# PSUM seeds in two blocks only, five staging buffers, earlier stores of differences, a merge over eight banks, and fetches issued one by one

## The chip, the cores and the metric

The kernel runs on one core of a Trainium2 chip. The metric is the time of one execution on the device, in microseconds (us), as the median of three runs. A profile of one more execution supplies everything else. The engines are TensorE (PE; PEld is its weight load), VectorE (DVE), ScalarE (ACT), GpSimd (POOL) and SyncE (SP). SP only issues DMAs here, and ACT issues some beside its computing. Each engine works through its own instruction list strictly in order, so an instruction that waits holds up all that stand behind it.

## The reference

A retention layer feeds two gated layers; all is in float32, for 3,072 tokens of 512 features.

```python
for t in range(S):
    state = gamma * state + einsum('bhd,bhe->bhde', k[:, :, t], v[:, :, t])
    y[:, :, t] = scale * einsum('bhd,bhde->bhe', q[:, :, t], state)
x = y.transpose(0, 2, 1, 3).reshape(3072, 512)
x = ((x @ w1) * (x @ w2) @ w3) @ w_out            # 512 -> 1024 -> 1024 -> 512
h = maximum(maximum(x @ u1, x @ u2), x @ u3)      # 512 -> 768
out = h @ u_out                                   # 768 -> 512
```

## The kernel before

Each matrix product is done by a seven-product scheme (Strassen's, in the Winograd form): an operand is cut into quarters, seven sums of quarters are multiplied, and sums of the seven products give the four quarters of the result. Each factor is split into a rounded value and a remainder (`hi`, `lo`), and three matmuls (hi·hi, hi·lo, lo·hi) make one product to near float32 accuracy. Those are the three lines L495, L496, L497, which always come together.

The stages in order of time, with their place in the profile: attention (0 to 88 us); the first gate, `x @ w1` times `x @ w2` (88 to 332, lines 473 to 545); the merge of `w3` and `w_out` into one matrix (332 to about 382, `merge_mm`); the product with it, "the x stage" (to 494, lines 640 to 690); the second gate with its maximum (494 to 763, lines 735 to 815); the last product.

**The first gate** runs over six blocks: two groups `g` of output columns, and in each the three token sets `n`; `blk = g * NB + n`. A block has seven steps `q`, and a step has four groups `p` of six matmuls into one PSUM bank each, so a block has 168 matmuls. `s = 7 * blk + q` counts the steps. `sets_b` gives the eight banks two names: set `a` takes steps 0, 2, 4, 6 and set `b` takes 1, 3, 5, and the two change places from block to block. Each group's result is taken out of PSUM after its last matmul:

```python
if q == 0:
    nc.scalar.copy(out=sets["b"][p] if blk else u, in_=ps)
elif seeded:
    nc.scalar.copy(out=u, in_=ps)
elif q == 1:
    nc.vector.tensor_tensor(out=u, in0=u, in1=ps, op=ALU.add)
```

So in block 0 step 0 is copied to the SBUF tile `U`, and step 1 is added to it by DVE (L504). In later blocks step 0 is copied by ACT (L500) into the banks that step 1 uses next, step 1 accumulates on top of it (a "seed"), and ACT copies the finished sum to `U` (L502). Steps 2 and 3 are copied to `C` and `E` by ACT (L506, L508), steps 4, 5 and 6 are combined by DVE (L510, L512, L517), and POOL multiplies `C` by `U` (L513). In steps 0 and 1 of the next block `fsums` forms four differences (`z` 0 to 3) of the finished quarters on DVE (L239), and `store` puts each on a list that `stores()` sends at the end of the step, from SP, to the scratch tensor `fsp`. Until such a store has landed, L506 and L508 may not overwrite `C` and `E`.

**Weights** come as 64-bit numbers and are turned into float32 on the chip. `fetch` starts the DMA of one weight tile (512 KB) into one of three staging tiles `stg`, and `step` alternates `decode_a` and `decode_b`: ACT L117, POOL L119, DVE L140 and L142, ACT L149, DVE L128 (or L134), ACT L130, DVE L108. A staging tile is free after L108 (L134), and only then `due_more` issues the next fetch, from ACT's queue (`late`). `Spread` deals these steps out evenly over the groups of a block, by `side.tick()`. `wgen` (lines 197 to 222) makes the seven sums of the second column group's weights, one at the end of each of seven steps, from step `s = 14 + LAG` on. `make_op` prepares the left operands in blocks 0 to 2; from block 3 on they are reloaded from the scratch tensor `opsp` by ACT's DMAs (L486, 1 MB each), three steps ahead.

**The merge** writes product `z` into `bank[z % 4]`, and two ACT copies (L586) take it out. **The second gate** has three rounds `j` of three blocks. Its operands are reloaded by L633, its seeds are L787, and at the start of a round `more(3)` starts three fetches for the next round.

Before each stage `more(3)` fills the three staging tiles.

Of the kernel before, what the change touches and what calls it, by code (L numbers as in the profile page):

```python
# [32 lines left out]
GA = 4  # L33
# [7 lines left out]
NSTG = 3  # L41
# [6 lines left out]
def fused_kernel(ctx: ExitStack, tc: tile.TileContext, ck, w12, w3t, wo1, w123, wo2, mask, gout, gch, kdec, out):  # L48
    nc = tc.nc
# [12 lines left out]
    fsp = dram.tile([NB, 7, 2, P, 2 * N], F32, name="fsp")  # L62
# [16 lines left out]
    stage_turn = [0]  # L79
    loaded, fronts, pending, wq = [], [], [], []  # L80

    def fetch(src, raw, hi=None, lo=None, st=None):
        k = stage_turn[0]
        stage_turn[0] += 1
        st = stg[k % NSTG][:, :] if st is None else st
        (nc.scalar if late[0] else nc.sync).dma_start(out=st.bitcast(I64), in_=src)
        loaded.append((st, dec_t[k % 2][:, :], raw, hi, lo))
# [81 lines left out]
    def store(dst, src, wait=1):  # L169
        later.append([wait, dst, src])  # L170
# [64 lines left out]
    def fsums(n, g, z):  # L235
        c, e = (work[nm] for nm in "CE")
        x00, x10, x01, x11, t = c[:, :1024], c[:, 1024:], e[:, :1024], e[:, 1024:], s_t[:, :]
        o, a, b, q = ((x00, x01, x00, 4), (t, x11, x00, 2), (x01, x11, x01, 3), (x10, t, x10, 5))[z]
        nc.vector.tensor_tensor(out=o, in0=a, in1=b, op=ALU.subtract)  # L239
        store(fsp[n, q, g], o, 0)  # L240

# [151 lines left out]
    with tc.manual_schedule():  # L393
# [72 lines left out]

        LAG = 3
        PB = (-1, -1, -1, -1, -1, -1, -1)
        wq += [lambda i=i, u=u: fetch_w12(i, u) for u in range(2) for i in range(GA, KF)]
        more(3)  # L470
        side = Spread([idle] * 5 + [step] * (4 * GA), 4 * (14 + LAG))
        wgen = weights(raw_quads(1024), 1024)
        for g in range(KF // GA):
            for n in range(NB):
                blk = g * NB + n
                sets = sets_b(blk)
                for q in range(7):
# [11 lines left out]
                    w = wslot(q).rearrange("p h (i k n) -> p h i k n", i=GA, k=2)  # L489
                    seeded = blk > 0 and q == 1  # L490
                    for p in range(GA):
# [7 lines left out]
                        if q == 0:  # L499
                            nc.scalar.copy(out=sets["b"][p] if blk else u, in_=ps)  # L500
                        elif seeded:
# [14 lines left out]
                        else:  # L516
                            nc.vector.tensor_tensor(out=e, in0=e, in1=ps, op=ALU.mult)  # L517
                            if p == GA - 1:
                                store(fsp[n, 6, g], work["E"][:, 1024:], 0)
                        side.tick()  # L520
                        if g == 0 and p == PB[q]:
# [8 lines left out]
                    if 0 <= z < 7:  # L530
                        wgen((0, 1, 4, 2, 3, 5, 6)[z])
                    if z == 6:
# [8 lines left out]
                               for k in range(2 * KF)]  # L541
                        more(3)
                        side = Spread([idle] * 3 + [step] * 36, 4 * (7 * NB - LAG))
# [31 lines left out]
        def merge_mm(z):  # L575
            ps = bank[z % 4]
            for k in range(KF):
# [156 lines left out]
        for j in range(GH):  # L734
# [5 lines left out]
            else:  # L740
# [6 lines left out]
                              + [lambda q=q: wogen(q) for q in (0, 1, 5, 2, 3, 4, 6)], 2 * 21 + 6)  # L747
            more(3)
            wgen = weights(raw_quads(256 * GH), 256 * GH)
            for n in range(NB):  # L750
# [3 lines left out]
                for q in range(7):  # L754
# [7 lines left out]
                    if j == GH - 1 and n == NB - 1:  # L762
                        if q == 3:
                            o_load(0, 0, 0)
                            o_load(0, 0, 1)
                        elif q == 4:
                            o_load(0, 1, 0)
                            o_load(0, 1, 1)
                        elif q == 5:
                            o_split(0)  # L770
                        elif q == 6:
                            o_split(1)
                            o_pre(2)
                    which, first = ORDER[q]
                    x = op_slot(s)
# [148 lines left out]
```

## Time and profile before

| | |
|---|---|
| median of 3 runs | 844.88 us (844.42 to 845.82) |
| the profiled execution, its own time | 846.29 us |
| its span, first to last instruction | 844.5 us |
| PE busy | 819.6 us, 97% |
| DVE busy | 628.7 us, 74% |
| ACT busy | 404.4 us, 48% |
| POOL busy | 116.2 us, 14% |
| mean granted TensorE clock | 0.997 of full speed |
| moved by DMA | 247.59 MB |

PE is busy nearly all the time, so the time is the sum of its matmuls and of the gaps between them. All other engines matter only where PE waits for them.

### The profile page before, as it was taken

How to read it: one execution, taken by the hardware profiler on the slowest of the kernel's cores; microseconds unless marked ns; L12 is line 12 of the kernel's file. 1: busy time of each engine (PE TensorE's matmuls, PEld its weight loads, DVE VectorE, ACT ScalarE, POOL GpSimd, SP SyncE). 2: the span in 40 equal slices, each digit the busy share in tenths (PEclk: the TensorE clock that was granted, in tenths of full speed). 3: DMA queues.
4: the chain of work that ended last, by engine and by line, in shares of the span. 5: the costliest groups of instructions: out<-in, count | busy, mean ns of one | idle time of the engine just before them, and what ended most of it. 6: DMA issues, size and time to landing. Idle time of an engine off the chain costs nothing.

```text
span 844.5 us, 12199 instructions
## 1 busy us (share of the span) xinstructions
PE 819.6 (97%) x4648; PEld 681.5 (81%) x4648; DVE 628.7 (74%) x746; ACT 404.4 (48%) x621; POOL 116.2 (14%) x119
## 2 busy tenths in 40 slices
PE   9999999999999989999999999999999999999998
PEld 8889787878877767878888878877888888887886
DVE  3899889787495858859889947896546564778793
ACT  2543545453445444557676624553343334335542
POOL 3443023231140404100110000100000010000000
PEclk9999999999999999999999999999999999999999
DMA  9996678787979994676788797869999899856522
GB/s 348 408 407 255 216 305 336 294 342 289 365 275 405 317 342 182 217 302 204 253 285 318 280 366 273 322 249 371 378 344 314 314 351 364 281 244 225 211 100 75
DMA packets 55499, 247.59 MB, mean 293 GB/s; under 512 B 6416, under 2 KB 6544, under 8 KB 40976
## 3 DMA queue, kind: packets, MB, share of 16 engines
q1 hardware_dynamic: 39456, 152.34, 46.8%
q10 hardware_dynamic: 15984, 94.47, 30.9%
q8 instruction: 37, 0.61, 0.3%
q14 instruction: 22, 0.18, 0.1%
HBM read 164.99 MB, written 81.79 MB: 292 GB/s over the span
## 4 chain that ended last, share of the span: by engine, by line
PE 52%; DMA 2%; DVE 2%; issue 1%; ACT 1%; POOL 0%; SPq 0%; ACTq 0%; DVEq 0%
PE bank L782 9%; PE bank L784 9%; PE bank L783 9%; PE bank L660 4%; PE bank L659 4%; PE bank L661 4%; PE bank L844 3%; PE bank L845 3%; PE bank L843 3%; DMA T<-hsp 1%; DMA op<-opsp 1%; PE bank L580 1%; PE bank L581 1%; PE bank L582 1%; DVE w L731 0%
## 5 line engine op out<-in xcount | busy, mean ns | idle before, releaser
L782 PE MATMUL bank<-op,w 128*128 128x512 f32 x378 | 147.5, 390 | 2.8 <-ACT bank L787 1.5
L784 PE MATMUL bank<-op,w 128*128 128x512 f32 x378 | 147.1, 389 | 0.0
L783 PE MATMUL bank<-op,w 128*128 128x512 f32 x378 | 147.1, 389 | 0.0
L495 PE MATMUL bank<-op,w 128*128 128x512 f32 x336 | 132.6, 395 | 11.0 <-ACT bank L500 8.8
L496 PE MATMUL bank<-op,w 128*128 128x512 f32 x336 | 131.6, 392 | 0.0
L497 PE MATMUL bank<-op,w 128*128 128x512 f32 x336 | 131.4, 391 | 0.0
L119 POOL TENSOR_SCALAR dec<-dec 128x512 f32<-128x512 f32 x64 | 49.0, 766 | 504.9 <-ACT dec L117 487.4
L495 PEld LDWEIGHTS bank<-op,w 128*128 128x128 f32 x336 | 63.4, 189 | 28.5 <-ACT bank L500 11.8
L782 PEld LDWEIGHTS bank<-op,w 128*128 128x128 f32 x378 | 71.0, 188 | 19.1 <-ACT bank L787 2.7
L783 PEld LDWEIGHTS bank<-op,w 128*128 128x128 f32 x378 | 71.0, 188 | 14.7
L784 PEld LDWEIGHTS bank<-op,w 128*128 128x128 f32 x378 | 71.0, 188 | 14.6
L149 ACT ACTIVATE dec<-stg 128x512 int32<-128x512 uint32 x59 | 39.9, 676 | 72.3 <-DVE stg L142 68.4
L497 PEld LDWEIGHTS bank<-op,w 128*128 128x128 f32 x336 | 63.5, 189 | 13.4
L496 PEld LDWEIGHTS bank<-op,w 128*128 128x128 f32 x336 | 63.4, 189 | 12.9
L659 PE MATMUL bank<-op,w 128*128 128x512 f32 x168 | 65.4, 389 | 0.0
L660 PE MATMUL bank<-op,w 128*128 128x512 f32 x168 | 65.4, 389 | 0.0
L661 PE MATMUL bank<-op,w 128*128 128x512 f32 x168 | 65.4, 389 | 0.0
L140 DVE TENSOR_SCALAR dec<-dec 128x512 int32<-128x512 int32 x64 | 35.2, 550 | 32.0 <-POOL dec L119 32.0
L117 ACT ACTIVATE dec<-stg 128x512 f32<-128x512 f32 x59 | 39.2, 664 | 22.0 <-DMA stg<-in_w3t_dram 11.4
L142 DVE SCALAR_TENSOR_TENSOR stg<-stg,dec 128x512 int32<-128x512 int32 x59 | 43.6, 739 | 4.4
L513 POOL TENSOR_TENSOR C<-C,U 128x512 f32<-128x512 f32 x24 | 37.7, 1591 | 45.9 <-DVE C L512 43.7
L795 DVE TENSOR_TENSOR m<-m,bank 128x512 f32<-128x512 f32 x34 | 23.2, 684 | 24.1 <-PE bank L784 23.4
(192 smaller groups left out, 1538.9 us busy)
## 6 DMA issues: line engine op xcount, KB each, us to landing
op<-opsp ACTq DMA_DIRECT2D x71, 1024.0 KB, 7.6
opsp<-op SPq DMA_DIRECT2D x34, 1024.0 KB, 4.9
ck<-in_ck_dram SPq DMA_DIRECT2D x48, 512.0 KB, 10.1
fsp<-C SPq DMA_DIRECT2D x24, 512.0 KB, 4.9
stg<-in_w3t_dram ACTq DMA_DIRECT2D x16, 512.0 KB, 3.9
hsp<-m SPq DMA_DIRECT2D x32, 256.0 KB, 6.6
stg<-in_w_dram SPq DMA_DIRECT2D x15, 512.0 KB, 9.7
stg<-in_w_dram ACTq DMA_DIRECT2D x14, 512.0 KB, 4.3
```

The source lines that it names most:

```text
L119: nc.gpsimd.tensor_scalar(out=df, in0=df, scalar1=MAX_HI, scalar2=MIN_HI, op0=ALU.min, op1=ALU.max)
L142: nc.vector.scalar_tensor_tensor(out=top, in0=top, scalar=-0x40000000, in1=dec, op0=ALU.bitwise_and, op1=ALU.bitwise_or)
L149: nc.scalar.activation(out=dec, in_=low.bitcast(U32), func=ACT.Copy, scale=2.0 ** -29)
L495: nc.tensor.matmul(ps, wh, x[:, 0, k, :], start=first and k == 0 and not seeded, stop=False, skip_group_check=True)
L496: nc.tensor.matmul(ps, wh, x[:, 1, k, :], start=False, stop=False, skip_group_check=True)
L497: nc.tensor.matmul(ps, wl, x[:, 0, k, :], start=False, stop=k == 1, skip_group_check=True)
L659: nc.tensor.matmul(ps, wh, x[:, 0, k, :], start=first and kk == 0 and k == 0, stop=False, skip_group_check=True)
L660: nc.tensor.matmul(ps, wh, x[:, 1, k, :], start=False, stop=False, skip_group_check=True)
L661: nc.tensor.matmul(ps, wl, x[:, 0, k, :], start=False, stop=kk == 1 and k == 1, skip_group_check=True)
L782: nc.tensor.matmul(ps, wh, x[:, 0, k, :], start=first and k == 0 and not seeded, stop=False, skip_group_check=True)
L783: nc.tensor.matmul(ps, wh, x[:, 1, k, :], start=False, stop=False, skip_group_check=True)
L784: nc.tensor.matmul(ps, wl, x[:, 0, k, :], start=False, stop=k == 1, skip_group_check=True)
```

## The change

It has five parts. (1) Only blocks 1 and 2 are seeded; in blocks 3 to 5 ACT copies step 0 to `U`, and DVE adds step 1. (2) The ring of staging tiles has five places in the first gate: the three `stg` and the two halves of `rwa`, which is taken out again before the last seven fetches. (3) `fsums` issues its store at once, and forms the difference in the second half of `C` before that in `E`. (4) The merge gives each product a bank of its own. (5) The three fetches at a round's start are issued at steps 0, 2 and 4 of its first block. With these go `LAG` 4 for 3 (the new weights are made one step later, 4 before 1), no decode ticks in step 0 of blocks 1 and 2, and `PB[0] = 3`, by which `make_op` of step 0 follows its matmuls in the lists.

```diff
@@ fetch
+    ring = [x[:, :] for x in stg]
...
-        st = stg[k % NSTG][:, :] if st is None else st
+        st = ring[k % len(ring)] if st is None else st
@@ fsums
-        o, a, b, q = ((x00, x01, x00, 4), (t, x11, x00, 2), (x01, x11, x01, 3), (x10, t, x10, 5))[z]
+        o, a, b, q = ((x00, x01, x00, 4), (t, x11, x00, 2), (x10, t, x10, 5), (x01, x11, x01, 3))[z]
         nc.vector.tensor_tensor(out=o, in0=a, in1=b, op=ALU.subtract)
-        store(fsp[n, q, g], o, 0)
+        nc.sync.dma_start(out=fsp[n, q, g], in_=o)
@@ first gate
-        LAG = 3
-        PB = (-1, -1, -1, -1, -1, -1, -1)
+        LAG = 4
+        SEED = (1, 2)
+        PB = (3, -1, -1, -1, -1, -1, -1)
...
-        more(3)
-        side = Spread([idle] * 5 + [step] * (4 * GA), 4 * (14 + LAG))
+        ring += [rwa[:, :1024], rwa[:, 1024:]]
+        stage_turn[0] = 0
+        more(5)
+        side = Spread([idle] * 5 + [step] * (4 * GA), 4 * (12 + LAG))
...
-                    seeded = blk > 0 and q == 1
+                    seeded = blk in SEED and q == 1
...
-                            nc.scalar.copy(out=sets["b"][p] if blk else u, in_=ps)
+                            nc.scalar.copy(out=sets["b"][p] if blk in SEED else u, in_=ps)
...
-                        side.tick()
+                        if g or q or not n:
+                            side.tick()
...
-                        wgen((0, 1, 4, 2, 3, 5, 6)[z])
+                        wgen((0, 4, 1, 2, 3, 5, 6)[z])
...
-                        more(3)
+                        wq[-7:-7] = [idle, lambda: ring.__delitem__(slice(3, 5))]
+                        more(5)
@@ merge_mm
-            ps = bank[z % 4]
+            ps = bank[z]
@@ second gate, for j in range(GH)
-            more(3)
...
+                    if n == 0 and q in (0, 2, 4):
+                        due[0] = 0
+                        more()
```

The line numbers of the changed kernel are higher by 1 to 9; in the pieces of it below L87 is the fetch (L86 before), L118 is L117, L131 is L130, L150 is L149, L178 is L177, L206 is L205, L214 is L213, L240 is L239, L490 is L486, L504 is the copy L500, and L508 is DVE's add L504.

On ACT, at the start of block 4, this stands before. The first four copies go into the banks of step 1; the rows between belong to the decoding of the weights.

```order
L500 COPY bank_1094<-bank_1090 128x512
L130 CAST wo_2_1992<-stg_60 128x512
L500 COPY bank_1095<-bank_1091 128x512
L500 COPY bank_1096<-bank_1092 128x512
L149 ACTIVATE dec_64<-stg_61 128x512
L117 ACTIVATE dec_63<-stg_62 128x512
L86 DMA stg_60<-in_wo_dram 128x512
L500 COPY bank_1097<-bank_1093 128x512
L486 DMA op_73<-opsp 128x2048
L502 COPY U<-bank_1094 128x512
L130 CAST wo_3_1993<-stg_61 128x512
L502 COPY U<-bank_1095 128x512
```

The same place in the changed kernel:

```order
L504 COPY U<-bank_1090 128x512
L131 CAST wo_1_2020<-rwa 128x512
L504 COPY U<-bank_1091 128x512
L150 ACTIVATE dec_63<-stg_60 128x512
L118 ACTIVATE dec_64<-stg_61 128x512
L87 DMA rwa<-in_wo_dram 128x512
L504 COPY U<-bank_1092 128x512
L504 COPY U<-bank_1093 128x512
L131 CAST wo_2_2021<-stg_60 128x512
L490 DMA op_73<-opsp 128x2048
L150 ACTIVATE dec_64<-stg_61 128x512
L118 ACTIVATE dec_63<-stg_62 128x512
```

The four copies now go to `U`, and ACT's four copies of step 1 (L502) are gone. The fetch behind L117 was for the tile that the next L117 reads; now it is for the third L117 after.

On DVE, from the end of block 2 into the first two steps of block 3 (`w_65` to `w_71` are the weights of steps 0 to 6), this stands before:

```order
L517 TENSOR_TENSOR E<-E,bank_1092 128x512
L517 TENSOR_TENSOR E<-E,bank_1093 128x512
L205 TENSOR_TENSOR w_67<-wraw,w_67 128x1024
L239 TENSOR_TENSOR C<-E,C 128x1024
L239 TENSOR_TENSOR s_t<-E,C 128x1024
L205 TENSOR_TENSOR w_68<-wraw,w_68 128x1024
L239 TENSOR_TENSOR E<-E 128x1024
L239 TENSOR_TENSOR C<-s_t,C 128x1024
L205 TENSOR_TENSOR w_70<-wraw,w_70 128x1024
L205 TENSOR_TENSOR w_71<-wraw,w_71 128x1024
```

The changed kernel has ahead of the piece the four L517, the remainder of `w_66` and two of three weight sums, and then:

```order
L214 TENSOR_TENSOR wraw<-wraw 128x1024
L240 TENSOR_TENSOR C<-E,C 128x1024
L240 TENSOR_TENSOR s_t<-E,C 128x1024
L206 TENSOR_TENSOR w_67<-wraw,w_67 128x1024
L508 TENSOR_TENSOR U<-U,bank_1090 128x512
L508 TENSOR_TENSOR U<-U,bank_1091 128x512
L240 TENSOR_TENSOR C<-s_t,C 128x1024
L508 TENSOR_TENSOR U<-U,bank_1092 128x512
L508 TENSOR_TENSOR U<-U,bank_1093 128x512
L240 TENSOR_TENSOR E<-E 128x1024
L206 TENSOR_TENSOR w_68<-wraw,w_68 128x1024
L206 TENSOR_TENSOR w_70<-wraw,w_70 128x1024
```

The remainders of the weights of steps 1, 2 and 3 have moved back behind the last L517, with the three weight sums; the four adds are new; and the difference in `C` stands ahead of that in `E`.

On SP, at the end of the x stage and the start of the second gate, this stands before (`rwa` and `rwb` hold operands on their way to scratch, `m` results of the first block):

```order
L177 DMA opsp<-rwa 128x2048
L177 DMA opsp<-rwb 128x2048
L86 DMA stg_61<-in_w_dram 128x512
L86 DMA stg_62<-in_w_dram 128x512
L86 DMA stg_60<-in_w_dram 128x512
L177 DMA hsp<-m_3805 128x512 x2
L177 DMA opsp<-op_73 128x2048
```

And this in the changed kernel:

```order
L178 DMA opsp<-rwa 128x2048
L178 DMA opsp<-rwb 128x2048
L87 DMA stg_62<-in_w_dram 128x512
L87 DMA stg_60<-in_w_dram 128x512
L178 DMA hsp<-m_3805 128x512
L87 DMA stg_61<-in_w_dram 128x512
L178 DMA hsp<-m_3805 128x512
```

Nothing of the second gate stands between the first two fetches; only the third is now behind a store of the first block's result.

## Rows read from the trace of the kernel before

**Rows 1.** PE's waits over the span: who for whom, total us, times, longest.

```profile
PE bank L580 <- ACT rwa L586: 2.1, 1, 2.1
PE bank L495 <- ACT C L506: 2.0, 1, 2.0
PE bank L782 <- ACT bank L787: 1.5, 2, 0.9
PE bank L782 <- DMA op<-opsp: 1.3, 1, 1.3
```

**Rows 2.** PE's waits for seeds in blocks 2, 4 and 5, one row each.

```profile
PE bank L495 <- ACT bank L500: 1.7, 2, 1.5
PE bank L495 <- ACT bank L500: 2.2, 2, 1.6
PE bank L495 <- ACT bank L500: 3.8, 2, 2.0
```

**Rows 3.** Windows of blocks 0, 4, 5: length; busy us (instructions) of PE, PEld, DVE, ACT, POOL; clock; DMA share; GB/s.

```profile
88.70:127.00 38.30, 38.21 (x168) 31.27 (x168) 32.34 (x35) 18.72 (x26) 5.20 (x5) 1.00 0.73 287
245.90:286.70 40.80, 38.63 (x169) 31.34 (x168) 29.23 (x44) 21.79 (x38) 9.42 (x12) 1.00 0.95 356
286.70:332.50 45.80, 40.02 (x168) 31.92 (x167) 32.28 (x47) 22.07 (x39) 10.84 (x12) 0.96 0.76 280
```

**Rows 4.** A window in block 5, same columns.

```profile
316.00:322.00 6.00, 4.41 (x12) 3.51 (x13) 2.71 (x5) 5.05 (x10) 0.61 (x1) 0.72 0.68 278
```

**Rows 5.** Timeline in block 5: start, us, engine, line; in brackets idle before, and releaser.

```profile
289.07 0.67 DVE L517 TENSOR_TENSOR E<-E,bank 128x512 f32<-128x512 f32 x1
...
292.90 0.66 ACT L130 CAST w<-stg 128x512 fp32r<-128x512 f32 x1 [3.08 <-DVE stg L128]
...
294.11 0.50 PE L495 MATMUL bank<-op,w 128*128 128x512 f32 x1 [1.96 <-ACT bank L500]
...
319.90 0.43 DVE L140 TENSOR_SCALAR dec<-dec 128x512 int32<-128x512 int32 x1 [0.58 <-POOL dec L119]
```

**Rows 6.** ACT's waits: block 4 (first row), block 5 (the other two).

```profile
ACT dec L117 <- DMA stg<-in_wo_dram: 8.1, 4, 2.7
ACT dec L117 <- DMA stg<-in_w3t_dram: 7.0, 3, 3.7
ACT C L506 <- DMA fsp<-C: 5.5, 1, 5.5
```

**Rows 7.** DVE's waits: block 4 (first row), block 5 (the other two).

```profile
DVE dec L140 <- POOL dec L119: 10.0, 7, 3.1
DVE dec L140 <- POOL dec L119: 7.0, 6, 4.0
DVE stg L128 <- ACT dec L149: 6.3, 1, 6.3
```

**Rows 8.** DVE's groups by line: count, busy us, mean ns, idle before and releaser.

```profile
L142 DVE SCALAR_TENSOR_TENSOR stg<-stg,dec 128x512 int32<-128x512 int32 x59 | 43.6, 739 | 4.4
L140 DVE TENSOR_SCALAR dec<-dec 128x512 int32<-128x512 int32 x64 | 35.2, 550 | 32.0 <-POOL dec L119 32.0
L128 DVE CUSTOM_DVE_ANT_0 stg<-stg,dec 128x1024 uint16<-128x1024 uint16 x24 | 17.7, 739 | 7.8 <-ACT dec L149 7.2
L512 DVE TENSOR_TENSOR C<-C,bank 128x512 f32<-128x512 f32 x24 | 15.4, 678 | 0.0
L108 DVE TENSOR_TENSOR w<-stg,w 128x512 fp32r<-128x512 f32 x10 | 8.3, 828 | 0.0
L239 DVE TENSOR_TENSOR E<-E 128x1024 f32<-128x1024 f32 x6 | 7.3, 1218 | 0.0
```

**Rows 9.** DMA issues over the span: count, KB each, median us from issue to landing.

```profile
op<-opsp ACTq DMA_DIRECT2D x71, 1024.0 KB, 7.6
stg<-in_w3t_dram ACTq DMA_DIRECT2D x16, 512.0 KB, 3.9
```

**Rows 10.** Timeline at the start of the second gate, columns as in rows 5.

```profile
482.24 2.44 SPq L86 DMA_DIRECT2D stg<-in_w_dram  x3
485.12 0.33 ACTq L633 DMA_DIRECT2D op<-opsp  x1
...
494.52 0.50 PE L782 MATMUL bank<-op,w 128*128 128x512 f32 x1 [1.28 <-DMA op<-opsp]
```

## The prediction

> **What bounds the kernel now.** I read the page first: PE is busy 97% of the span, so only what makes PE wait can pay. The second view is PE's waits [rows 1, 2]. It shows that the waits sit in four places: the seeds of the first gate, one wait for `C`, the merge, and the start of the second gate. The third view is the windows by block [rows 3]: block 0 has 168 matmuls in 38.3 us and no wait, block 4 takes 40.8 and block 5 takes 45.8, so these two lose 2.5 + 7.5 = 10.0 us. A block has 28 groups, so a group is 38.3 / 28 = 1.37 us and a step 5.47.
>
> In blocks 4 and 5 PE waits 2.2 + 3.8 us for seeds and 2.0 for L506 [rows 1, 2]. Right behind the last of these the granted clock is 0.72 over 6 us [rows 4], a stretch partly at 1.2 GHz instead of 2.4; before it fell, PE had stood still for 2.0 us, and for 1.96 us and more some 20 us earlier [rows 1, 5]. It costs 6 × 0.28 = 1.7 us. Together 9.7, which agrees with the windows' 10.0.
>
> The waits of ACT and DVE say why [rows 6, 7]. ACT stands at L117 for 8.1 us in block 4 and 7.0 in block 5, because the weight tile has not landed; POOL's L119 follows, DVE waits at L140 (10.0 and 7.0 us), ACT then waits for DVE, and the seed copy L500 is queued behind. [Rows 5] show such a moment: ACT idles 3.08 us for L128, then come its queued instructions, and PE idles 1.96. A seed is the tightest deadline: the copy of a group must be done three groups after that group, 4.1 us. Without it a bank is free as soon as its reader is through, two steps less a group later: 2 × 5.47 − 1.37 = 9.6 us.
>
> **The change part by part.**
>
> *Blocks 3 to 5 unseeded, five staging tiles, the store at once.* Removed per block: four L500 into PSUM and four L502; added: four copies to `U` on ACT and four adds on DVE. PE no longer waits for ACT at step 1 but for L517 alone. In block 5 L517 ran at 289.07 [rows 5] for a group that ended at about 286.7 − 5.47 + 1.37 = 282.6: 6.5 us late of 9.6, so 3.1 are left, and the seeds' 6.0 us go even if DVE stays as late. The wait for L506 ends with the landing of the store of `C`, 5.5 us of idle ACT [rows 6]. That difference was the fourth and is the third (one L239 earlier, 1.2 us [rows 8]), and DVE was held ahead of it by a wait for a weight tile, of which the longest is 3.7 [rows 6]. Earlier by 1.2 + 3.7 is more than PE's 2.0. A fetch now has three decodes to land where it had one. A decode is paced at 2 × 68 / 39 = 3.5 groups, 4.8 us, so the lead goes from 4.8 to 14.3 us, against a median landing of 3.9 [rows 9]. I take all of the 9.7 (bounds: the 2.0 and 1.7 stay, so 6.0; or the windows' 10.0).
>
> *What it loads on DVE.* This is the price. Per block: 4 adds and 12 other passes out of PSUM, 16 × 0.68 = 10.8; four differences, 4 × 1.22 = 4.9; and eight decodes (39 jobs over 68 groups, 28 groups a block, two jobs each) of 0.55 + 0.74 + 0.74 + 0.83 = 2.86, so 22.9 [rows 8]. That is 38.6 of 38.3 us: DVE is full, before it has waited at all. What DVE waits, w us a block, adds up over blocks 4 and 5 and reaches PE once the 3.1 us are used: 2 × (0.3 + w) − 3.1. Today w is 10.0 and 13.3 [rows 7]. With tiles there in time what is left is the round through ACT and POOL; 0.58 us at L140 where nothing else was late [rows 5], at most 8 × 0.58 = 4.6 a block, and nothing where DVE is behind and its inputs lie ready. I take w = 2: a loss of 1.5 (bounds 0 and 6.7).
>
> *LAG 4.* The weights of steps 2 and 3 of block 3 are now made behind the last L517 of block 2. From there to the remainder of step 3's weight DVE has, in order, a remainder, three sums, two differences, a remainder, two adds, a difference, two adds, a difference and a remainder: ten passes of 1,024 columns, counted as 1.22 each like the differences [rows 8], and four adds. That is 10 × 1.22 + 4 × 0.68 = 14.9, after a start about 0.7 into block 3, so 15.6 us; the matmuls of step 3 begin at 3 × 5.47 = 16.4. Step 2's remainder is ready at 0.7 + 7 × 1.22 = 9.2, needed at 10.9. Both fit, by 0.8 and 1.7. If DVE arrives as late as 6.5 us, 5.7 us show. Nothing holds DVE there (the decoding has paused, and the sums stand behind L512 and L517, no longer ahead of them), so I take 0.3.
>
> *Ticks left out of step 0 of blocks 1 and 2, and PB.* They keep decode work from between the seed copies. Block 2 has two waits of 1.7 in all, the longest 1.5 [rows 2]; the short one, 0.2, goes. The 1.5, and its like in block 1, stay: the copy there waits for L517, and what DVE does ahead of L517 is the same number of instructions as before.
>
> *Merge over eight banks.* Product 4 no longer waits for the copy of product 0: 2.1 us [rows 1]. ACT is no earlier, but the next use of a copy's result, the split of `rwa` for the x stage, lies behind product 3 and has the four last products as cover. I take 2.1 (bounds 0, if the x stage's first weights then are late, and 2.1).
>
> *Fetches one by one.* At the second gate's start the operand's load is issued at 485.12 and PE waits for it until 494.52, 1.3 us too long [rows 1, 10]. It takes 9.4 us where the median is 7.6 [rows 9], with three fetches issued ahead of it from 482.24. But SP's order shows that the first two fetches still stand together: SP is not held by the steps of PE, so only one of three leaves its way. I take 0.9 (bounds 0 and 1.3). The two waits for seeds of the second gate, 1.5 [rows 1], I leave as they are (bound: the 0.9 of the longer one, at the start of a round, goes too).
>
> Sum: 9.7 + 0.2 + 2.1 + 0.9 − 1.5 − 0.3 = 11.1 us, of the profiled execution's 846.29, so 835.2. The median of the runs is 1.4 lower, and the same gain gives 844.88 − 11.1 = **833.8 us**.
>
> A rule stands against the fetches. [Rows 3] have the DMA engines busy for 0.95 of block 4 and 0.76 of block 5, 38.8 + 34.8 = 73.6 us of full share, where the two blocks are to take 76.6. The Trainium skill, *DMA: Bandwidth & Descriptors*, section "Issuing engines are not separate DMA queues", says that DMAs of all issuing engines run on the same 16 engines and interleave. By it a deeper ring buys no bandwidth and its extra fetches stand ahead of operand loads and stores of `C`; the trace agrees as far as [rows 10] go. By the row the sum stays as it is, with 3 us to spare; by the rule in full the case "DMA crowded" below would hold.
>
> **The rivals.**
>
> *DVE stays behind a little (chance 0.13).* w = 4.6, every decode makes its round: 6.7 lost for 1.5, the gain is 5.9, 839.0 us. For it: DVE's load of 38.6. Against it: inputs lie ready when DVE is late.
>
> *DMA crowded (0.10).* Five fetches at once in front of block 3's end and shorter blocks keep the engines full, so that a store of `C` lands late in both blocks, as in block 5 now: twice 2.0 + 1.7 = 7.4 of the 11.1 go, 841.2 us. For it: the shares above. Against it: the store starts earlier by about 5 us.
>
> *Slower: DVE's waits stay (0.08).* The adds are put on a DVE that waits as today, 10.0 and 13.3: it loses 0.6 + 23.3 − 3.1 = 20.8 for 1.5, 844.88 − 11.1 + 19.3 = 853.1 us. It decides from the w at which the rest of the sum, 12.6, equals 2 × (0.3 + w) − 3.1, so 7.5 us a block. For it: 6.3 of today's wait comes from ACT standing at L506, not from a fetch [rows 6, 7]. Against it: the rest goes back to L117.
>
> *The spaced fetches do nothing* (they hardly are spaced): 0.9 less, 834.7, inside the forecast's own spread.
>
> **How the numbers follow.** My forecast has 0.65, with a spread of its own from 830.5 (all bounds good: 10.0 + 0.2 + 2.1 + 1.3 + 0.9 = 14.5, nothing lost, 830.4) to 837. DVE a little behind has 0.13, DMA crowded 0.10, slower 0.08, and 0.04 is for no measurable change. A measurement of this kernel can tell about 0.2%, 1.7 us, so "same" is 843.2 to 846.6. Faster: 0.65 + 0.13 + 0.09 = 0.87; same 0.05; slower 0.08. The range of 8 in 10 is 830.3 to 841.3: it takes in the forecast, the first rival and part of the second.
>
> **What the profile will show.** Right: no wait of PE for L500's line in blocks 4 and 5 and none for L506, a clock of 1.00 there, windows of 38 to 39.5 us; L117's waits for DMA near nothing; DVE busy for over 90% of blocks 4 and 5; no wait in the merge; the wait of 1.5 in block 2 and its like in block 1 unchanged. Wrong, if PE waits for DVE's L504, L510, L512 or L517 in blocks 4 and 5 (DVE full), for a weight in block 3 (LAG), or for L506 once more (DMA); or if the x stage begins no earlier after the merge.

## The result, and the profile after

The change takes 832.9 us as the median of 4 runs (831.8 to 834.0) against 845.4 (844.4 to 848.8) for the kernel before on the same chip: a ratio of 0.985, 95% interval 0.981 to 0.988, so 12.4 us less. The forecast was 833.8. The execution that was profiled took 833.7 us, with a span of 831.9. The total came out nearly as forecast; the terms behind it did not. The table takes each stage from its first matmul to the first of the next, in the two profiled executions, in us.

| stage | before | after | saved | forecast |
|---|---|---|---|---|
| block 0 | 38.6 | 38.2 | 0.4 | 0 |
| block 1 | 39.6 | 39.7 | -0.1 | 0 |
| block 2 | 40.6 | 38.4 | 2.2 | 0.2 |
| block 3 | 38.2 | 38.1 | 0.1 | -0.3 |
| block 4 and block 5 | 40.8 + 46.4 | 38.1 + 44.2 | 4.9 | 9.7 - 1.5 |
| merge | 45.9 | 43.5 | 2.4 | 2.1 |
| x stage, to the second gate's first matmul | 115.7 | 114.5 | 1.2 | 0.9 |
| second gate, and what follows | 350.0 | 348.8 | 1.2 | 0 |

With 0.2 us ahead of block 0 that makes the 12.6 us by which the spans differ.

I read the kernel after in the order of the prediction. First PE's waits over the span (who for whom, total us, times, longest), which answer to [rows 1]:

```profile
PE bank L499 <- ACT E L512: 2.0, 1, 2.0
PE bank L499 <- ACT bank L504: 1.3, 1, 1.3
...
PE bank L790 <- ACT bank L795: 1.2, 2, 0.7
PE bank L499 <- ACT C L510: 0.6, 1, 0.6
...
PE bank L499 <- DVE E L521: 0.2, 1, 0.2
```

The lines have moved by 1 to 9: L499 is a matmul of the first gate, L504 the copy after step 0, L510 and L512 the copies to `C` and `E`, L521 DVE's last product. The merge's wait and the one for an operand at the second gate's start are gone, and so are the seeds' waits of block 2, which I had expected to stay, as well as those of 4 and 5; the 1.3 us for L504 are block 1's alone. Of the 2.0 us for `C`, 0.7 are left (the 0.6 and one of 0.1), and there are 2.0 us for `E`. The windows, which answer to [rows 3, 4], are blocks 0, 2, 4 and 5, and then eight microseconds in block 5:

```profile
88.40:126.60 38.20, 38.20 (x170) 31.66 (x169) 32.65 (x36) 19.12 (x26) 5.10 (x4) 1.00 0.81 317
166.31:204.75 38.44, 38.37 (x169) 31.47 (x168) 32.55 (x37) 17.32 (x27) 12.37 (x8) 1.00 0.80 308
242.83:280.91 38.08, 38.08 (x169) 31.55 (x168) 31.83 (x46) 18.90 (x33) 8.84 (x10) 1.00 0.87 341
280.91:325.10 44.19, 41.16 (x169) 32.34 (x168) 36.30 (x53) 20.79 (x36) 12.23 (x12) 0.96 0.73 284
310.00:318.00 8.00, 5.98 (x20) 4.48 (x19) 4.30 (x8) 4.93 (x9) 1.23 (x2) 0.79 0.36 149
```

Block 4 is now without a gap. Block 5 is 6.1 us longer than it: PE waits 3.0 (the 2.0, the 0.6, the 0.2 and one of 0.1) and is busy 3.1 longer, of which the granted clock of 0.79 behind the wait for `E`, a stretch partly at 1.2 GHz instead of 2.4, makes 8 × 0.21 = 1.7. This dip belongs to the profiled execution: its mean granted clock is 0.998, that of the other three runs 1.000. DVE is busy 84% of block 4 and 82% of block 5, not over 90%. The timeline shows where the wait for `E` begins:

```profile
302.36 1.22 DVE L240 TENSOR_TENSOR E<-E 128x1024 f32<-128x1024 f32 x1
...
303.61 0.32 SPq L241 DMA_DIRECT2D fsp<-E  x1
...
311.86 0.59 ACT L512 COPY E<-bank 128x512 f32<-128x512 f32 x1 [3.42 <-DMA fsp<-E]
312.50 0.50 PE L499 MATMUL bank<-op,w 128*128 128x512 f32 x1 [2.02 <-ACT E L512]
```

The difference is ready at 303.6 and its store is sent at once, but the copy that may overwrite `E` starts at 311.9, 8.2 us later. Over the span the median of stores out of `E` is 5.9, and of those out of `C` 3.7, the blocks' products included (issues: count, KB each, median us to landing):

```profile
fsp<-C SPq DMA_DIRECT2D x24, 512.0 KB, 3.7
...
fsp<-E SPq DMA_DIRECT2D x12, 512.0 KB, 5.9
```

Of the waits behind [rows 6, 7], ACT waits for no weight tile any more in blocks 4 and 5. What DVE still waits for in the two blocks is the round through ACT and POOL, 13.3 us in five rows, of which these are the largest:

```profile
DVE stg L129 <- ACT dec L150: 4.4, 1, 4.4
DVE rwa L129 <- ACT dec L150: 2.9, 1, 2.9
DVE dec L141 <- POOL dec L120: 2.2, 4, 0.6
```

### The profile page after: what moved, and what is told of

It is laid out like the page before. It is cut to its first block, busy times and chain, and to the rows that moved or that the text cites. A ratio compares the mean times of both kernels' runs of the same rounds, so it can differ in the third digit from the quotient of the medians.

```text
span 831.9 us, 12196 instructions
## 1 busy us (share of the span) xinstructions
PE 817.4 (98%) x4648; PEld 681.7 (82%) x4648; DVE 636.6 (77%) x758; ACT 398.3 (48%) x609; POOL 116.3 (14%) x119
## 4 chain that ended last, share of the span: by engine, by line
PE 58%; DMA 3%; DVE 2%; ACT 0%; issue 0%; ACTq 0%; DVEq 0%
PE bank L790 9%; PE bank L791 9%; PE bank L792 9%; PE bank L665 4%; PE bank L666 4%; PE bank L667 4%; PE bank L852 3%; PE bank L853 3%; PE bank L851 3%; PE bank L586 2%; PE bank L587 2%; PE bank L588 2%; DMA opsp<-op 2%; DMA fsp<-E 1%; DMA op<-opsp 1%; PE bank L499 1%
## 5 line engine op out<-in xcount | busy, mean ns | idle before, releaser
L499 PE MATMUL bank<-op,w 128*128 128x512 f32 x336 | 132.5, 394 | 4.4 <-ACT E L512 2.0
L500 PE MATMUL bank<-op,w 128*128 128x512 f32 x336 | 131.5, 391 | 0.0
L499 PEld LDWEIGHTS bank<-op,w 128*128 128x128 f32 x336 | 63.5, 189 | 20.6 <-ACT E L512 2.4
L500 PEld LDWEIGHTS bank<-op,w 128*128 128x128 f32 x336 | 63.6, 189 | 12.8
L150 ACT ACTIVATE dec<-stg 128x512 int32<-128x512 uint32 x49 | 33.1, 677 | 47.4 <-DVE stg L143 43.4
L141 DVE TENSOR_SCALAR dec<-dec 128x512 int32<-128x512 int32 x64 | 37.1, 579 | 23.7 <-POOL dec L120 23.7
L517 POOL TENSOR_TENSOR C<-C,U 128x512 f32<-128x512 f32 x24 | 36.1, 1524 | 71.2 <-DVE C L516 64.7
L852 PE MATMUL bank<-w,wo 128*128 128x512 f32 x96 | 37.5, 390 | 0.0
L143 DVE SCALAR_TENSOR_TENSOR stg<-stg,dec 128x512 int32<-128x512 int32 x49 | 34.6, 707 | 3.7
```

The lines of the kernel that those rows point to most:

```text
L141: nc.vector.tensor_scalar(out=dec, in0=dec, scalar1=3, scalar2=0x3FFFFFFF, op0=ALU.logical_shift_left, op1=ALU.bitwise_and)
L499: nc.tensor.matmul(ps, wh, x[:, 0, k, :], start=first and k == 0 and not seeded, stop=False, skip_group_check=True)
L500: nc.tensor.matmul(ps, wh, x[:, 1, k, :], start=False, stop=False, skip_group_check=True)
L852: nc.tensor.matmul(ps, wh[:, k, o], xl[:, k], start=False, stop=False, skip_group_check=True)
```

## The experiments

All kernels were timed in five rounds against the kernel before on the same chip; "first gate" is the time from its first matmul to the merge's, in the profiled execution: 244.3 us before, 236.7 after. The runs come from three chips, on which the kernel before has medians of 845.1 to 846.2. Runs of one changed kernel lie 2 to 8 us apart, so a difference of under 2 us between two medians is read from the traces alone, and each trace is one execution.

**Seeds in all blocks again.**

```diff
-        SEED = (1, 2)
+        SEED = (1, 2, 3, 4, 5)
```

> The change as it is, but with the first gate's blocks 3 to 5 seeded in PSUM again (SEED = 1 to 5); five tiles, differences, merge and fetches stay. Theory A, my prediction's step (a seed is the tightest deadline, 4.1 us, and DVE runs 6 to 7 us behind PE in blocks 4 and 5): PE waits for the seed copy's line again, 2 us or so in each of blocks 4 and 5, with a granted clock under 0.9 behind it; about 837 us (835 to 840). Theory B, the wait came from late weight tiles alone and the five tiles cure it: no seed wait in blocks 4 and 5, and DVE has 2.7 us a block less to do, so the wait for L512 in block 5 goes too; 830 to 833 us.

It took 834.2 us, ratio 0.986 (0.983 to 0.990), first gate 236.3. Block 4 is 38.1 us without a wait, so theory A fails there. In block 5 PE waits for a seed:

```profile
PE bank L499 <- ACT bank L504: 3.8, 1, 3.8
```

That is what A said, and larger. No weight tile is late there: ACT waits for none in blocks 4 and 5. DVE is late (its last product of block 4 ends 8.4 us into block 5), and the seed copy (L504) stands in ACT's list behind a fetch that leaves when DVE has freed its tile:

```profile
288.19 0.68 DVE L109 TENSOR_TENSOR w<-stg,w 128x512 fp32r<-128x512 f32 x1
...
288.90 0.34 ACTq L87 DMA_DIRECT2D stg<-in_w3t_dram  x1
...
289.91 0.57 ACT L504 COPY bank<-bank 128x512 f32<-128x512 f32 x1 [1.59 <-DMA fsp<-C]
```

The profile puts the last 1.6 us to a store of `C`; whether that or the fetch held the copy is not settled. After the change the same copy, to `U`, starts no earlier (290.31), and PE does not feel it. But with the seeds the waits for `E` and `C` are gone in exchange, and block 5 takes 43.8 us for 44.2. Taking the seeds out is worth nothing that the times show while five tiles are there.

**Three staging tiles again.**

```diff
-        ring += [rwa[:, :1024], rwa[:, 1024:]]
-        stage_turn[0] = 0
-        more(5)
+        more(3)
...
-                        wq[-7:-7] = [idle, lambda: ring.__delitem__(slice(3, 5))]
-                        more(5)
+                        more(3)
```

> The change as it is, but with three staging tiles for fetches instead of five (the ring is not lengthened, three fetches are sent off at once, nothing is deleted from it later). Theory A (a fetch needs the lead of three decodes): ACT waits for weight tiles at L118's line again, 7 us or so a block, DVE waits behind it, and since DVE has no slack in blocks 4 and 5 most of that comes out at PE: 838 us or more. Theory B (taking the seeds away is enough, since a bank then has 9.6 us): DVE waits, but PE does not, 832 to 834 us. Theory C (the DMA engines are crowded, and fewer fetches ahead let the store of E land sooner): the 2.0 us for L512 in block 5 shrink, 830 to 832 us.

835.4 us, ratio 0.989 (0.985 to 0.992), first gate 235.5. ACT's waits for weights are back (blocks 4 and 5):

```profile
ACT dec L118 <- DMA stg<-in_w3t_dram: 7.7, 4, 3.1
ACT dec L118 <- DMA stg<-in_wo_dram: 7.4, 4, 3.7
```

PE hardly feels them: block 4 stays at 38.1 us without a wait, and block 5 takes 43.4, with 3.4 us of waits in all for 3.0 after the change. What is lost is lost elsewhere: the x stage takes 117.0 for 114.5, with three waits of PE at its start, 1.9 us, for operands and a weight. So A had the wait right and its price wrong, and B holds in the first gate. C has a point: `E`'s store lands sooner, 6.2 us from issue to copy for the 8.2 after the change, and PE waits 0.1 us for it, but 1.6 for `C`'s copy.

```profile
305.95 0.32 SPq L241 DMA_DIRECT2D fsp<-E  x1
...
312.14 0.59 ACT L510 COPY E<-bank 128x512 f32<-128x512 f32 x1 [2.19 <-DMA fsp<-E]
```

Five tiles or no seeds: either one keeps block 4 clean.

**The differences as before, in order and in time of store.**

```diff
-        o, a, b, q = ((x00, x01, x00, 4), (t, x11, x00, 2), (x10, t, x10, 5), (x01, x11, x01, 3))[z]
+        o, a, b, q = ((x00, x01, x00, 4), (t, x11, x00, 2), (x01, x11, x01, 3), (x10, t, x10, 5))[z]
...
-        nc.sync.dma_start(out=fsp[n, q, g], in_=o)
+        store(fsp[n, q, g], o, 0)
```

> The change as it is, but with the four differences of a block in the order of before (the one that ends in C last) and stored at the end of a step instead of at once. Theory A (C's bank is wanted one step, 5.5 us, before E's, so that what is stored last decides): the wait of 2.0 us for E's copy in block 5 goes, and PE waits for C's copy instead, 4 to 7 us with a dip of the clock behind it; 836 to 840 us. Theory B (with five tiles and no seeds either order leaves the same last landing and so the same wait, by another name): 2 us for C's copy, 832 to 834 us.

846.2 us, ratio 1.001 (0.999 to 1.004): with this one small edit undone the whole gain is gone, and the first gate takes 247.8 us, 3.5 more than before. ACT and PE, first gate:

```profile
ACT C L510 <- DMA fsp<-C: 38.8, 6, 8.5
...
PE bank L499 <- ACT C L510: 6.6, 2, 4.8
...
PE bank L499 <- ACT bank L504: 4.2, 2, 2.9
```

Theory A has the direction, but even its 840 was too low: PE waits in blocks 1, 2, 4 and 5, not in 5 alone. Theory B is out.

**The two halves of that edit, one at a time.** First the old order, stored at once:

```diff
-        o, a, b, q = ((x00, x01, x00, 4), (t, x11, x00, 2), (x10, t, x10, 5), (x01, x11, x01, 3))[z]
+        o, a, b, q = ((x00, x01, x00, 4), (t, x11, x00, 2), (x01, x11, x01, 3), (x10, t, x10, 5))[z]
```

> The change as it is, but with the differences in the order of before (C's upper half last); they are still stored at once. The run with both halves of this edit undone took 846.2 us, 13 us more than the change. Theory A (the order carries it: the copy into C's upper half is due one step before the copy into E's lower half, and ACT stands before it until the store has landed): 843 to 847 us, PE waits of 4 to 5 us for C's copy in block 5 and of 2 to 3 us for a seed in block 2. Theory B (the store at the end of a step carries it, since the operand's store of 1 MB and the end of the step then stand ahead of it): 832 to 835 us.

Then the new order, stored at the end of the step:

```diff
-        nc.sync.dma_start(out=fsp[n, q, g], in_=o)
+        store(fsp[n, q, g], o, 0)
```

> The change as it is, but with the differences stored at the end of a step as before; their order stays the new one (E's lower half last). Theory A (the order carries the 13 us): 832 to 834.5 us, at most one wait of 2 to 3 us for E's copy in block 5. Theory B (the time of the store carries them): 842 to 847 us. If each does half: 836 to 841 us in this run and in the one with the old order alone.

The old order takes 841.0 us, ratio 0.993 (0.991 to 0.996); the late store 838.0, ratio 0.989 (0.986 to 0.992). So each does a part, 8.1 and 5.0 us more than the change; both together did 13.3. (The first gate, in the traces, is longer by 6.6 and 3.5, and by 11.1 with both.) They work at different places. With the old order `C`'s store is sent last, at 307.76, and its landing stops ACT, then PE, in block 5 (timeline of the run with the old order):

```profile
307.76 0.32 SPq L241 DMA_DIRECT2D fsp<-C  x1
...
316.15 0.59 ACT L510 COPY C<-bank 128x512 f32<-128x512 f32 x1 [6.83 <-DMA fsp<-C]
...
316.79 0.80 PE L499 MATMUL bank<-op,w 128*128 128x512 f32 x1 [4.22 <-ACT C L510]
```

8.4 us from issue to copy, about as for `E` after the change (8.2). But the bank that this copy frees is used again in step 4, and that of `E`'s copy in step 5, a step of 5.47 us later. With the late store the damage is done in block 1 and shows in block 2. Here is SyncE's queue, then ACT, DVE and PE, in the run with the late store:

```profile
142.88 0.32 SPq L178 DMA_DIRECT2D opsp<-op  x1
144.02 0.35 SPq L178 DMA_DIRECT2D fsp<-C  x1
...
150.52 1.07 ACT L510 COPY C<-bank 128x512 f32<-128x512 f32 x2 [7.16 <-DMA fsp<-C]
...
152.57 1.23 DVE L249 TENSOR_TENSOR op<-xr,op 128x1024 fp32r<-128x1024 f32 x1 [4.64 <-ACT op L248]
...
174.13 2.47 DVE L521 TENSOR_TENSOR E<-E,bank 128x512 f32<-128x512 f32 x4
...
175.52 0.50 PE L499 MATMUL bank<-op,w 128*128 128x512 f32 x1 [2.88 <-ACT bank L504]
```

and the same places after the change:

```profile
140.19 0.38 SPq L178 DMA_DIRECT2D opsp<-op  x1
143.60 0.32 SPq L241 DMA_DIRECT2D fsp<-C  x1
...
146.97 1.07 ACT L510 COPY C<-bank 128x512 f32<-128x512 f32 x2 [4.03 <-DMA fsp<-C]
...
149.02 1.23 DVE L249 TENSOR_TENSOR op<-xr,op 128x1024 fp32r<-128x1024 f32 x1 [1.51 <-ACT op L248]
...
170.60 2.46 DVE L521 TENSOR_TENSOR E<-E,bank 128x512 f32<-128x512 f32 x4
...
171.36 2.36 ACT L504 COPY bank<-bank 128x512 f32<-128x512 f32 x4 [4.71 <-DVE E L521]
```

With the late store the operand's store of 1 MB (`opsp`) goes 1.1 us ahead of `C`'s; `C`'s is through 6.5 us after its issue, against 3.4 where the 1 MB left earlier. (That the 1 MB is the reason is not shown by itself; the DMA engines are full, at a share of 1.0, in both runs.) ACT stands at L510, the operand's rounding L248 is queued behind it, DVE waits for that, and 20 us later DVE's last product of block 1 (L521) is 3.5 us late (174.13 for 170.60), the seed behind it too, and PE stops for 2.9 us. A wait of ACT in one block is paid by PE in the next.

**The numbers ahead of block 3 as before.**

```diff
-        LAG = 4
-        PB = (3, -1, -1, -1, -1, -1, -1)
+        LAG = 3
+        PB = (-1, -1, -1, -1, -1, -1, -1)
...
-                        if g or q or not n:
-                            side.tick()
+                        side.tick()
...
-                        wgen((0, 4, 1, 2, 3, 5, 6)[z])
+                        wgen((0, 1, 4, 2, 3, 5, 6)[z])
```

> The change as it is, but with the numbers of before ahead of block 3: LAG 3, PB -1 in all steps, ticks in step 0 of blocks 1 and 2, and the weights in the order 0, 1, 4. Theory A (block 2's 2.2 us came from the ticks and the operand's place, which let DVE come to the seeds' adds sooner): block 2 takes 40.5 us instead of 38.4, PE waits for the seed there again, 834.5 to 835.5 us. Theory B (it came from the five fetches sent off at once, which keep ACT from waiting for a tile): block 2 stays at 38.4 us, 832.5 to 833.5 us. By either theory block 3 stays within 0.4 us of 38.1.

831.1 us, ratio 0.984 (0.981 to 0.988), first gate 233.4. Block 2 stays free of waits (38.1 us) and block 3 at 38.1: theory A is out, the numbers did not free block 2. Nor did the five tiles of theory B alone, since the two runs before this one have them too, and wait there, while the run with three tiles has block 2 at 38.1 us; it was the differences. Block 0 goes back to 38.6 us, so these numbers (I didn't separate them) give the 0.4 there. Of PE's waits in blocks 4 and 5 one is left (the second row is the window of block 5):

```profile
PE bank L499 <- ACT E L512: 2.6, 1, 2.6
...
280.81:321.82 41.01, 38.40 (x170) 31.45 (x169) 32.82 (x48) 19.21 (x34) 9.46 (x10) 1.00 0.74 284
```

The wait is longer than the 2.0 us after the change, yet the clock stays at 1.00 and block 5 takes 41.0 us for 44.2. So the dip of the clock does not always follow such a wait, and most of the 3.3 us between the two first gates is PE's busy time in block 5, 38.4 for 41.2.

This is the shortest median of all, but its interval overlaps that of the change, so it is no proof that `LAG` 4 costs anything.

**The kernel before with the differences alone:**

```diff
-        o, a, b, q = ((x00, x01, x00, 4), (t, x11, x00, 2), (x01, x11, x01, 3), (x10, t, x10, 5))[z]
+        o, a, b, q = ((x00, x01, x00, 4), (t, x11, x00, 2), (x10, t, x10, 5), (x01, x11, x01, 3))[z]
...
-        store(fsp[n, q, g], o, 0)
+        nc.sync.dma_start(out=fsp[n, q, g], in_=o)
```

> The kernel before with one edit alone: the differences in the new order and stored at once; seeds in all blocks, three tiles, LAG 3, merge over four banks and bursts of fetches as before. Theory A (this edit is the main part of the change, since undoing seeds or the ring alone costs 1 to 3 us and undoing this costs 13): the first gate's blocks 4 and 5 and block 2 lose most of their 11 us of waits, 834.5 to 838.5 us. Theory B (it only keeps the deeper ring and the unseeded blocks from making things worse; by itself it takes away the 2.0 us for C's copy in block 5 and the 1.7 us of clock behind it): 840.5 to 842.5 us, with the seeds' waits of 2.2 and 3.8 us in blocks 4 and 5 still there.

840.1 us, ratio 0.992 (0.989 to 0.995), first gate 236.2: as short as after the whole change, with seeds everywhere and three tiles. Blocks 2 and 4 take 38.1 and 38.6 us, as theory A wanted; yet the total is theory B's, because the merge now takes 50.1 us instead of 45.9. The waits of PE over the span, and the window of the merge:

```profile
PE bank L495 <- ACT bank L500: 4.7, 4, 2.7
...
PE bank L580 <- ACT rwa L586: 3.9, 1, 3.9
```

```profile
324.84:374.93 50.09, 46.21 (x194) 37.71 (x193) 34.75 (x47) 22.20 (x41) 9.54 (x10) 0.93 0.67 250
```

**The two late parts undone in the change.**

```diff
-            ps = bank[z]
+            ps = bank[z % 4]
...
+            more(3)
...
-                    if n == 0 and q in (0, 2, 4):
-                        due[0] = 0
-                        more()
```

> The change as it is, but with the two late parts undone: the merge over four banks and three fetches at once at the start of a round of the second gate; they show at different places of the trace. My prediction's steps: 2.1 us for the copy of product 0 come back in the merge, and 0.9 to 1.3 us at the start of the second gate for the operand's load; 835.9 to 836.3 us. Theory B (the merge's wait depends on how late ACT is, and ACT is now earlier by the copies of the unseeded blocks): the wait in the merge stays away, only the 1.3 come back, 834 us. Theory C (the operand's load is not held by the fetches): only the 2.1 come back, 835 us.

839.3 us, ratio 0.991 (0.988 to 0.994): 3 us more than my steps said. PE's waits from the merge on:

```profile
PE bank L586 <- ACT rwa L592: 3.8, 1, 3.8
PE bank L788 <- DMA op<-opsp: 1.1, 1, 1.1
```

The 1.1 us are the second gate's, as expected. The merge takes 49.2 us for 43.5: 3.8 of wait and 1.7 of clock behind it (0.70 and 0.88 over two windows of 4 us, 4 × 0.30 + 4 × 0.12). The copy of product 0 stands in ACT's list behind the decoding that the first gate leaves over. Here is PE at product 4, before and in this run:

```profile
362.39 0.50 PE L580 MATMUL bank<-wo,op 128*128 128x512 f32 x1 [2.09 <-ACT rwa L586]
...
355.33 0.62 PE L586 MATMUL bank<-wo,op 128*128 128x512 f32 x1 [3.78 <-ACT rwa L592]
```

The first gate ends 8.7 us sooner than before (324.19 for 332.94), but the copy lets PE go on only 7.1 us sooner. The 1.7 us by which the decoding does not follow are added to the 2.1, and the clock comes on top.

**Three small edits on the kernel before:** the differences as in the run above, and these; seeds, tiles and `LAG` as before.

```diff
-            ps = bank[z % 4]
+            ps = bank[z]
...
-            more(3)
...
+                    if n == 0 and q in (0, 2, 4):
+                        due[0] = 0
+                        more()
```

> The kernel before with three edits alone: the differences in the new order and stored at once, the merge over eight banks, the fetches of the second gate one by one. Seeds in all blocks, three tiles, LAG 3 and the ticks stay as before. Theory A (seeds, ring and LAG are worth almost nothing once the differences come in the new order, and the merge gives back what comes out of the first gate if it has four banks): 840.1 less 6.6 in the merge and 1.3 at the second gate's start, 831.5 to 833.5 us, with 1 to 3.5 us of seed waits left in block 5. Theory B, my prediction's (the seeds and the ring carry most of the 9.7 us of blocks 4 and 5): 836 to 841 us, with waits for seeds in blocks 4 and 5 as before.

835.3 us, ratio 0.988 (0.984 to 0.991), between the two theories. The merge is at 43.5 us and the second gate's start without a wait. The first gate, 238.6, keeps PE's waits for seeds, and ACT's for weights (from block 4 on):

```profile
PE bank L495 <- ACT bank L500: 6.7, 4, 2.0
```

```profile
ACT dec L117 <- DMA stg<-in_w3t_dram: 12.2, 8, 3.4
ACT dec L117 <- DMA stg<-in_wo_dram: 8.8, 4, 3.6
```

Of the 6.7 us, 1.2 are block 1's and 5.5 are in blocks 4 and 5, near the 6.0 of [rows 2]. The run with the differences alone has the same first gate by its code and waited 3.5 us there: such is the spread between executions. So late tiles do bring waits for seeds, as I had argued. Taking the seeds out removes those of blocks 4 and 5; five tiles alone remove block 4's, but not block 5's (3.8 us in the run with seeds in all blocks). That is the smaller part. In a row: 845, with the differences 840, with merge and fetches 835, with tiles and without seeds 831, with `LAG` 4 and its company 833.

**No decode ticks in step 0 of blocks 4 and 5**, on top of `LAG` 3:

```diff
-                        side.tick()
+                        if not g or q or not n:
+                            side.tick()
...
-                        side = Spread([idle] * 3 + [step] * 36, 4 * (7 * NB - LAG))
+                        side = Spread([idle] * 3 + [step] * 36, 4 * (7 * NB - LAG) - 8)
```

> The change with LAG 3 and the order of before ahead of block 3 (the run that took 831.1 us), and with no decode tick in step 0 of blocks 4 and 5 (the other steps take its jobs, 39 over 64 ticks in place of 72). Theory A (what is left in block 5, 2 to 2.6 us before E's copy, is DVE some 6 us behind: four ticks less ahead of the differences take one decode, 2.9 us, from before them): the wait goes, first gate 229 to 231 us, total 828 to 829.5 us. Theory B (the wait is the store's landing of 8 us on full DMA engines, and the fetches are now denser): the wait stays or grows, 831 to 834 us.

834.1 us, ratio 0.986 (0.983 to 0.989), no gain. The wait for `E` is nearly gone, but another came, 11 us ahead of the place where it stood with `LAG` 3 alone (PE's waits, block 5):

```profile
PE bank L499 <- DMA op<-opsp: 1.2, 1, 1.2
PE bank L499 <- ACT E L512: 0.2, 1, 0.2
```

So the wait was moved, not cured: the copy to `E` starts 29.2 us into block 5, for 29.3 with `LAG` 3 alone, and PE only arrives there later. Theory A is out. From 293 to 309 us the DMA share is 1.01 to 1.03, as theory B had it; but with `LAG` 3 alone it is 1.00 to 1.03 in the same stretch, so the pause did not fill the engines. What differs is when ACT issues the load of that operand: 9.7 us into block 5, for 5.7. The first gate is 233.3 us, as without the pause, in the shortest of the six executions.

**The same, with a seed in block 2 alone:**

```diff
-        SEED = (1, 2)
+        SEED = (2,)
```

> As the run before it, and with a seed in block 2 alone instead of blocks 1 and 2. Theory A (the 1.2 us in block 1 are the seed copy behind DVE's product, so without it half goes or all of it): 0.6 to 1.3 us less than the run before it. Theory B (PE then waits for the same product of DVE itself, and DVE has four adds more, 2.7 us, ahead of its work for the operands): the same time or up to 1.5 us more.

835.1 us, ratio 0.988 (0.985 to 0.991): theory B. Block 1's wait halves (0.6 us), and block 2 takes 40.5 us again, with 1.8 us of waits for its seed. In block 5 PE waits 2.4 us at step 3, whose operand's load ACT had issued still later, 10.3 us into the block; the profile names DVE's difference in `E` there, so the cause is not settled.

## Why the prediction was right in sum and wrong in parts

The total is right by luck as much as by working. Against the forecast, blocks 4 and 5 gave 3.3 us less (4.9 for 9.7 − 1.5), while block 2 gave 2.0 more, the last stages 1.2 and block 0 0.4, none of them foreseen; the rest is small.

*Blocks 4 and 5, 9.7 us:* mis-sized, 4.9 measured net of all losses. Block 4 gave its 2.8 in full, and the seeds' waits are gone in both. The step that failed is "Earlier by 1.2 + 3.7 is more than PE's 2.0". `C` came earlier, and its wait fell from 2.0 to 0.7, but I did not ask of the store that is now last when it lands and who needs it: `E`'s difference ends at 303.58, its landing takes 8.2 us, and PE waits 2.0 us, in this execution with the same dip of the clock. That is the mechanism of the rival "DMA crowded", in block 5 alone and for `E`. The bound of 6.0 that I gave (the 2.0 and 1.7 stay) was the better value.

*The cause of those waits* was half right. With late tiles the seeds' waits are there (three small edits, 5.5 us left), and without seeds they are gone; but with five tiles and no late one, block 5 still waits 3.8 us for a seed. That bears out the tight deadline of a seed, and neither part carries the change: undoing one costs 1 to 3 us by the medians, undoing the order and time of the differences 13. I had weighed that edit as one L239, 1.2 us, and part of 2.0.

*"The 1.5, and its like in block 1, stay"* was wrong for block 2, which gave 2.2. I had counted the instructions of DVE ahead of L517, which are the same, and not what DVE waits for among them: ACT, which stood at the copy to `C` behind a store's landing. The runs with each half undone show it (1.2 and 2.9 us of wait in block 2).

*DVE full, a loss of 1.5:* too dear by the load. I had 38.6 us a block; DVE was busy 31.8 in block 4. Its rows overlap: four products of 0.68 each take 2.47 above (L521), not 2.72, so 52 instructions cost some 4 us less than the sum of their durations, and only 46 ran in block 4 (53 in block 5). Its waits were too small in my sum: 13.3 us in the two blocks, where I had taken 2 each. By my formula that would have cost 2 × 0.3 + 13.3 − 3.1 = 10.8, so two errors went against each other. DVE is late all the same (the differences of block 4 end 22.7 us into block 5), which is why `E`'s store is. Of DVE's own products PE waited 0.2 for one.

*LAG, 0.3 of loss:* none in block 3 (38.1 us). What `LAG` does further on stays open.

*Merge, 2.1:* 2.4. The size fits the kernel before; as a part of this change it is worth 5.7, since it keeps a part of the first gate's gain from being lost there. I had not asked what becomes of this wait when PE arrives earlier and the decoding does not follow in full.

*Fetches, 0.9 of 1.3:* all 1.3 went, and 1.1 come back with the burst. That two of the fetches stand together did no harm.

*Not foreseen and not explained:* a wait of 0.7 us at the start of the last product is gone in every run, with the new differences or the old.

The Trainium skill, *DMA: Bandwidth & Descriptors*, section "Issuing engines are not separate DMA queues", says that DMAs of all issuing engines run on the same 16 engines and interleave. What I drew from it against five tiles came in part: `E`'s store takes 8.2 us to land, and 6.2 in the run with three tiles, in one execution each (the kernel before has 7.5, for `C`'s). The price of 7.4 that I gave to "DMA crowded" did not come, and block 4 has no wait.

## What to carry to other kernels

When a copy may overwrite a buffer only after its store has landed, count back from the copy: the buffer that is needed first is to be stored first, and as soon as it is ready, and what stands behind that copy on its engine pays with it, even a block later. A part of what is gained by removing a wait can be lost again at the next place where a slower stream (here the decoding) is awaited, so such places are to be mended together, and a part's worth in the old trace is not its worth in the new one. Before busy times are added up into a load, look whether neighbouring rows of the engine overlap.

## What was not expected of the hardware

A store of 512 KB took 3.4 us to land where the 1 MB ahead of it on its queue had left 3.4 us earlier, 6.5 us where it had left 1.1 us earlier, and 8.2 and 8.4 us in block 5, 6.2 there with three staging tiles. Rows of DVE that follow each other without a wait overlap by 0.08 us, so durations alone overstate its load by a tenth (2.72 for 2.47 above). A wait of PE of 2.0 us was followed by a stretch partly at 1.2 GHz in one execution, and one of 2.6 us at the same place in another was not.
